# Bias of the fourth attention block added by VectorE instead of by identity matmuls, with a new order of the work

## The chip, the cores and the metric

One core of one Trainium2 chip runs the whole kernel. The metric is the device time of one launch in microseconds (us).

## The reference, cut to what matters

```python
# q, k, v: 4 x 8 heads x 768 x 64; 8 global keys, 96 local ones
scores = scale * np.matmul(q, k.transpose(0, 1, 3, 2))
bias = -slopes[:, None, None] * dist[None, :, :]          # ALiBi-like, per head
scores = np.where(keep, scores + bias, -1e9)              # local band and global keys
a = softmax(scores);  x = a @ v                           # -> 3072 x 512
h = x @ w_in                                              # 512 x 2048: "first product"
out = softplus(h) @ w_out                                 # 2048 x 512: "second product"
```

Attention runs in 24 blocks of 128 queries, each against its own 128 keys and the 128 before (the first block of a sequence against its own alone). The two products run in 12 groups of 256 tokens; group g needs blocks 2g and 2g+1.

## The kernel before: what the change and the argument touch

The kernel is one list of small pieces of work, called ops here. A planner inside it gives each op a duration, a rank and its buffers, and lets the engines take ready ops by rank; the resulting list is emitted, and from then on each engine's order is fixed. `RANKS`, `BASE` and the `slack` of transfers steer the planner. A block with index below `EARLY` gets its bias on TensorE, a later one on VectorE:

```python
def bias_in(n, half, s_t):                    # TensorE: bias into PSUM
    for e in range(2):
        nc.tensor.matmul(s_t[:, 4*e:4*e+nr, :], ident[:],
                         bias[:, half, nr*e:nr*e+nr, :], start=True, stop=False)

def add_bias(n, half, s_t):                   # VectorE: PSUM + bias -> z in SBUF
    nc.vector.tensor_tensor(packed(n, z), rows_of(n, s_t), bias, ALU.add)
# ... (cut)
if n < EARLY:
    bi = pl.add(f"bias{n}{half}", "pe", 0.43 if i else 0.22, ...)
    sc = pl.add(f"scores{n}{half}", "pe", ...)          # adds onto the bias in PSUM
    ex = pl.add(f"exp{n}{half}", "act", 1.05, ...)      # reads PSUM
else:
    sc = pl.add(f"scores{n}{half}", "pe", ...)
    ab = pl.add(f"bias{n}{half}", "dve", 1.22, ...)     # scores + bias
    ex = pl.add(f"exp{n}{half}", "act", 1.05, ...)      # reads z
```

After the exponential come pv (times v, TensorE), norm (VectorE), TX (a transpose, TensorE) and TXout (a copy of the transposed block to XT, by VectorE or ScalarE). TX writes one of the two PSUM banks `h_ps` of the first product (or `o_ps`), so TXout both gives the products their input and frees a bank. ScalarE's exponential of a first product's result frees its bank, and its logarithm then makes the input `g` of the second product. `gv` are two small copies of global v rows, on VectorE, per half block at first and per block from block 4 on. And w_in comes in four slices, each of which serves two of a group's eight first products; the third slice is issued only at about 24 us.

The softmax here doesn't subtract the row's maximum and nothing guards it: scores larger than these inputs give would overflow.

## Time and profile before

| | before |
|---|---|
| time, median of 3 runs | 217.98 us (217.66 to 218.1) |
| span of the profile | 216.0 us |
| TensorE / VectorE / ScalarE busy | 97% / 56% / 72% |
| first product starts | 19.39 us |
| TensorE waits over 0.15 us after that | none |

The lines that carry this are in the prediction. One view is added here: the busy time of each engine in the stretch from 19.4 to 33 us (columns: stretch, its length, then busy us and count of instructions of TensorE, its weight loads, VectorE, ScalarE and GpSimd, then clock, DMA share and GB/s).

```profile
19.40:33.00 13.60, 13.60 (x148) 10.53 (x149) 8.48 (x21) 11.38 (x17) 4.80 (x7) 1.00 1.11 224
```

### The profile page before, as it was taken

Reading aid. Unit: us, or ns where it says so; the run is one execution under the profiler, and the core shown is the slowest. Engines: PE = TensorE matmul, PEld = TensorE weight load, DVE = VectorE, ACT = ScalarE, POOL = GpSimd, SP = SyncE. Lnnn points to the kernel's source line nnn. Section 1 sums busy time; section 2 is a strip of 40 time slices with the busy share of each in tenths; the row PEclk is TensorE's granted clock in tenths of the full one; section 3 lists DMA queues with packets and bytes.
Section 4 is the critical chain, followed back from the end, with each engine's and each line's share of the span. In section 5 each row is a group of like instructions: output and inputs, shape, how many; then the busy total and the mean of one; then the engine's idle time right before and its main releaser. Section 6 shows DMA issues by size and latency. Waiting matters only on the chain.

```text
span 216.0 us, 5102 instructions
## 1 busy us (share of the span) xinstructions
PE 210.3 (97%) x2060; PEld 146.1 (68%) x2060; DVE 122.0 (56%) x258; ACT 156.4 (72%) x208; POOL 65.2 (30%) x125
## 2 busy tenths in 40 slices
PE   8898999999999999999999999999999999999994
PEld 7576786766675767677767767666666766676643
DVE  6888664578837784883653854653774763111020
ACT  2667988887785869979869669749859768766530
POOL 3642710023965090560523271460550000000000
DMA  5999999999996999698988457767963211410112
GB/s 182 328 227 206 267 192 203 272 287 294 232 170 148 319 119 253 164 148 198 153 213 246 133 134 227 210 102 179 261 77 97 74 28 49 76 42 6 52 49 97
DMA packets 69879, 36.24 MB, mean 168 GB/s; under 512 B 28512, under 2 KB 67680, under 8 KB 69856
## 3 DMA queue, kind: packets, MB, share of 16 engines
q1 hardware_dynamic: 64528, 28.39, 57.5%
q0 software_dynamic: 5184, 7.34, 15.9%
q8 instruction: 16, 0.26, 0.6%
q10 hardware_dynamic: 144, 0.20, 0.3%
q14 instruction: 7, 0.06, 0.1%
HBM read 27.26 MB, written 6.29 MB: 155 GB/s over the span
## 4 chain that ended last, share of the span: by engine, by line
PE 91%; DMA 3%; DVE 2%; ACT 1%; SPq 1%; issue 0%
PE h_ps L591 40%; PE o_ps L619 32%; PE s_ps L492 6%; PE x_ps L547 5%; DMA q<-in_q_dram 3%; PE s_ps L644 3%; PE s_ps L619 3%; PE o_ps L732 1%; PE h_ps L418 1%; PE s_ps L477 1%; DVE vb L401 1%; DVE kb L370 0%; SPq L358 0%; PE o_ps L644 0%; PE x_ps L544 0%
## 5 line engine op out<-in xcount | busy, mean ns | idle before, releaser
L591 PE MATMUL h_ps<-XT,w_in_bf 128*128 128x256 bf16 x768 | 95.9, 273 | 0.8 <-DVE rcp L558 0.7
L591 PEld LDWEIGHTS <-w_in_bf 128*128 128x128 bf16 x768 | 72.9, 98 | 19.5 <-issue 1.1
L602 ACT ACTIVATE e<-h_ps 128x512 f32<-128x512 f32 x96 | 58.8, 629 | 33.8 <-PE h_ps L591 33.3
L619 PE MATMUL o_ps<-w_out_bf,g 128*128 128x512 bf16 x320 | 79.6, 379 | 0.0
L610 ACT ACTIVATE g<-e 128x1024 bf16<-128x1024 f32 x48 | 50.6, 1054 | 0.8
L619 PEld LDWEIGHTS <-g 128*128 128x128 bf16 x352 | 32.1, 98 | 26.1
L523 DVE TENSOR_TENSOR z<-s_ps,biasA 128x1024 f32<-128x1024 f32 x34 | 40.6, 1220 | 14.5 <-PE s_ps L492 13.9
L529 ACT ACTIVATE pb<-z 128x1024 bf16<-128x1024 f32 (+1 forms) x40 | 39.3, 984 | 7.0 <-DVE z L523 6.9
L558 DVE RECIPROCAL rcp<-x_ps 128x4 f32<-128x4 f32 x47 | 8.5, 180 | 37.9 <-PE x_ps L547 35.7
L663 DVE COPY osb<-o_ps 128x512 f32<-128x512 f32 x20 | 13.7, 685 | 23.6 <-PE o_ps L619 23.5
L401 POOL CAST vb<-v 64x512 bf16<-64x512 f32 (+1 forms) x39 | 23.4, 601 | 5.9 <-DMA v<-in_v_dram 3.9
L401 POOL CAST kb<-k 64x512 bf16<-64x512 f32 x32 | 20.6, 644 | 15.0 <-DMA k<-in_k_dram 13.7
L559 DVE TENSOR_TENSOR xs<-x_ps,rcp 128x256 bf16<-128x256 f32 x47 | 19.9, 424 | 1.6
L547 PEld LDWEIGHTS <-pb 128*128 128x128 bf16 x320 | 14.7, 97 | 3.4
L547 PE MATMUL x_ps<-vb,pb 128*128 128x65 bf16 x312 | 15.9, 193 | 0.0
L461 POOL COPY kT<-kT 128x32 bf16<-128x32 bf16 x12 | 2.5, 209 | 36.2 <-PE s_ps L492 26.7
L492 PEld LDWEIGHTS <-kT 64*128 64x128 bf16 x288 | 8.3, 94 | 7.5 <-issue 7.4
L669 POOL DMA_DIRECT2D out_dram<-osb x12 | 6.8, 568 | 18.7 <-DVE osb L663 16.8
L470 DVE COPY vb<-vb 4x512 bf16<-4x512 bf16 (+1 forms) x36 | 11.8, 328 | 0.5
L492 PE MATMUL s_ps<-qT,kT 64*128 64x128 bf16 x288 | 12.0, 218 | 0.0
L732 PE MATMUL o_ps<-zeros 128*128 128x128 bf16 x84 | 8.7, 261 | 1.4 <-DVE zeros L687 1.0
L533 ACT ACTIVATE pb<-s_ps 128x1024 bf16<-128x1024 f32 (+1 forms) x8 | 7.4, 920 | 3.0 <-PE s_ps L492 3.0
(79 smaller groups left out, 111.5 us busy)
## 6 DMA issues: line engine op xcount, KB each, us to landing
q<-in_q_dram SPq DMA_DIRECT2D x8, 512.0 KB, 5.6
k<-in_k_dram SPq DMA_DIRECT2D x8, 512.0 KB, 7.3
v<-in_v_dram SPq DMA_DIRECT2D x7, 512.0 KB, 7.9
out_dram<-osb POOLq DMA_DIRECT2D x12, 256.0 KB, 4.5
out_dram<-osb SPq DMA_DIRECT2D x11, 256.0 KB, 2.1
v<-in_v_dram SPq DMA_DIRECT2D x10, 256.0 KB, 3.4
w_in_bf<-in_moe_w_in_dram POOLq DMA_DIRECT2D x4, 512.0 KB, 8.8
w_out_bf<-in_moe_w_out_dram POOLq DMA_DIRECT2D x4, 512.0 KB, 11.7
```

The source lines that it names most:

```text
L401: copy_on[eng](dst[64 * r : 64 * r + 64, hs, :], src)
L470: nc.vector.tensor_copy(vb_of(n - 1)[sl, hs, 0:D], vb_of(first)[sl, hs, 0:D])
L492: nc.tensor.matmul(s_t[:, 4 * sub + (lh // 2 if i == 0 else 2 * (lh // 2) + b), :], k_of(n - b, rows, m), q_of(n, rows, m), start=begin, s ...
L523: nc.vector.tensor_tensor(packed(n, z), rows_of(n, s_t), bias, ALU.add)
L529: nc.scalar.activation(pb[:, 0:nr, :], z[:, 0:nr, :], AF.Exp, scale=1.0 / root_d)
L547: nc.tensor.matmul(xv[:, lh, :], pb[:, 2 * j + b, :], vb_of(n - b)[:, h, :], start=b == 0, stop=b == 1,)
L559: nc.vector.tensor_tensor(xs[:, 4 * half : 4 * half + 4, :], xv[:, :, 0:D], rcp[:][:, :, None].to_broadcast([P, 4, D]), ALU.mult,)
L591: nc.tensor.matmul(hv[:, j, :], w_in_bf[:, m, fb * P : fb * P + P], XT[:, m, W * g : W * g + W], start=(m == 0), stop=(m == NM - 1),)
L602: nc.scalar.activation(e[:, p % 2, :].rearrange("p (a t r) -> p a r t", a=4, r=2), state["h", g, p][:].rearrange("p (a r t) -> p a r t", a ...
L610: nc.scalar.activation(gt[:, 4 * c : 4 * c + 4, :].rearrange("p a t -> p (a t)"), state["e", g, c][:].rearrange("p a t -> p (a t)"), AF.Ln ...
L619: nc.tensor.matmul(dst, state["g", g][:, fb, ns * P : ns * P + P], w_out_bf[:, fb, :], start=(fb == 0), stop=(fb == NFB - 1),)
L663: copy_on[eng](osb[:], src)
```

## The change

The intent: take 0.86 us of matmuls that only add a bias off the full engine and give them to an engine with idle time. The diff, cut to its core:

```diff
 RANKS = {
-    ... 43 entries ...
+    ... 52 others ...
 }
-EARLY, MERGED, T_DMA, X_DMA = 4, 6, 4, 6
+EARLY, MERGED, T_DMA, X_DMA = 3, 6, 4, 6
-BASE = (-29.37, -38.43, -34.65, -17.24, 5.3, 14.23, -7.79, -35.22, 17.37, ...)
+BASE = (-42.8, -42.7, -41.18, -41, -13.51, 14.08, 7.53, -8.91, 17.37, ...)
-            slack=2.5 if w >= 4 else 0.0,                 # loads
+            slack=2.2 if w >= 4 else 0.0,
-            ... slack=2.4 ...                             # both transposes by DMA
+            ... slack=2.0 ...
```

## The prediction

> **What bounds the kernel now.** I read the head of the page first, to see which engine has no idle time. The three rows are busy time, then the busy tenths of 40 slices of 5.4 us.
>
> ```profile
> PE 210.3 (97%) x2060; PEld 146.1 (68%) x2060; DVE 122.0 (56%) x258; ACT 156.4 (72%) x208; POOL 65.2 (30%) x125
> PE   8898999999999999999999999999999999999994
> DVE  6888664578837784883653854653774763111020
> ```
>
> TensorE is at nine tenths in every slice but the first three (8, 8, 9, 8) and the last. VectorE has its densest stretch in slices 2 to 4 (5 to 22 us), and much room later. Busy alone proves little for TensorE, since matmuls overlap in the record, so next I read the waits of TensorE from 19.4 to 206 us, and then the mean step from the start of one matmul to the next in the timeline. The waits have one line in all:
>
> ```profile
> PE h_ps L591 <- DVE rcp L558: 0.7, 1, 0.7
> ```
>
> That is the wait that ends at 19.39 us, where the first matmul of the feed-forward part starts. After it TensorE never waits. The steps agree: the first product (128x256) takes 0.109 us a matmul and the second (128x512) 0.216 us, all through. So from 19.39 us on the time is the sum of the TensorE work that is left: the last matmul piece starts at 212.16 and runs 0.91, so the matmuls end at 213.07, and 213.07 - 19.39 = 193.7 us are saturated. The rest of the 216.0 us span is a tail of 2.9 us (copy and store). Everything that this change can win lies in two places: less TensorE work after 19.39 us, or a better use of the time before it.
>
> The second place I read from the timeline of TensorE (start, duration, what ran):
>
> ```profile
> 15.25 0.39 PE L732 MATMUL o_ps<-zeros 128*128 128x128 bf16 x4
> 15.57 0.40 PE L492 MATMUL s_ps<-q_first,k_first 64*128 64x128 bf16 x8
> ...
> 17.47 0.59 PE L477 MATMUL s_ps<-biasA,ident 128*128 128x512 bf16 x2
> 17.90 0.41 PE L547 MATMUL x_ps<-vb,pb 128*128 128x65 bf16 x8
> 18.24 0.40 PE L492 MATMUL s_ps<-q_first,k_first 64*128 64x128 bf16 x8
> 19.39 1.03 PE L591 MATMUL h_ps<-XT,w_in_bf 128*128 128x256 bf16 x8 [0.75 <-DVE rcp L558]
> 20.26 0.41 PE L547 MATMUL x_ps<-vb,pb 128*128 128x65 bf16 x8
> 20.50 0.59 PE L477 MATMUL s_ps<-biasA,ident 128*128 128x512 bf16 x2
> 20.93 0.41 PE L547 MATMUL o_ps<-vb,pb 128*128 128x65 bf16 x8
> ```
>
> L732 are fillers: products of zeros that keep TensorE awake and yield nothing. Between the first useful data (6.15) and 19.39 us I add the steps taken up by fillers: 0.27, 0.90 (with a gap in it), 0.24, 0.35, 0.42, 0.17, 0.32, 0.33, 0.29, 0.32 = 3.61 us. Add the idle pieces before 8.39 (0.44) and before 19.39 (0.75): 4.8 of these 13.24 us are no work. They are not free for the taking: each is there because the next block's data had not come through its casts, copies and exponentials. What they say is that before 19.4 us the limit is latency, and that it runs through VectorE: the chain of waits has VectorE pieces back to back from 16.35 to 19.34 us, where it does two casts of v, two small copies and then the copy to XT that the first product waits for.
>
> **What the Trainium skill says.** "TensorE: Matmul & The Clock Gate", Back-to-back issue gap, gives 518 cycles for N = 512 and 262 for N = 256, at 2.4 GHz: 0.216 and 0.109 us. The trace agrees: the bias matmuls step by 0.215, the two products by 0.216 and 0.109. "VectorE: DVE Perf Modes", The TRN2 errata, gives (N + 151)/0.96 ns for an fp32 add of two tensors, 1224 ns for N = 1024; the trace has 1220 ns for the same add of scores and bias. "Perfetto Trace Analysis", Optimization Strategy, notes that a kernel can have several regimes whose most-contended engine changes; here these are the 19.4 us of latency and the 194 us of TensorE.
>
> **The change part by part.** EARLY goes from 4 to 3, so the block with index 3 no longer gets its bias by matmuls.
>
> 1. *Removed from TensorE.* Each half has two 128x512 bias matmuls: 2 x 0.215 = 0.43 us, 0.86 us for both. The group has 12 such matmuls, six calls: blocks 1, 2 and 3, two halves each. By order of start the last two, at 17.47 and 20.50 us, are block 3's. The one at 20.50 lies in the saturated stretch: **-0.43 us** goes straight to the end. The one at 17.47 lies before the 0.75 us wait, and by itself would only lengthen that wait. It counts only if the new order puts other useful work there, or if the order has moved block 3 past the wait; I give it half, **-0.2 us**.
>
> 2. *Added to VectorE.* Two adds of scores and bias. The group that does it for the later blocks:
>
> ```profile
> L523 DVE TENSOR_TENSOR z<-s_ps,biasA 128x1024 f32<-128x1024 f32 x34 | 40.6, 1220 | 14.5 <-PE s_ps L492 13.9
> ```
>
> 2 x 1.22 = 2.44 us. ScalarE's exponential stays as it is, about 1.0 us, reading the sum from SBUF and not from PSUM. Block 3's scores come at 18.24 and 21.27 us in the kernel before. Counting busy time, VectorE has 2.1 us idle in 20 to 25, 1.25 in 25 to 30 and 2.7 in 30 to 35 us, so 2.44 us fit once the first product has started. Before 19.4 us it has little: 3.7 busy of 4.9 us from 14.5 to 19.4. If the add falls there, ahead of the XT copies of blocks 0 and 1, the first product starts up to 1.22 us later per add, and TensorE then has only fillers to run.
>
> 3. *Latency of block 3.* One VectorE step more per half, about 1.3 us. Block 3's output is needed only for the second group of the first product. The eight pieces of group 0 start at 19.39, 21.84, 22.77, 23.88, 27.26, 28.58 (two of them) and 30.76; group 1 starts only at 34.91. Block 3's transpose runs at 24.87, ten us early. The latency is hidden: 0.
>
> 4. *Moved.* All base times of the first eight blocks and nearly all ranks change, so this is another order, planned for the new work. The first four blocks get times well ahead of everything (-43 to -41), blocks 6 and 7 move back. The margins for DMA landings in the plan shrink (2.4 to 2.0, 2.5 to 2.2 us). I expect the order to win some of the 4.8 us: the 0.75 us wait, or a few fillers by bringing block 3's work before the first product. A search had been made for the kernel before too, so I estimate **-0.6 us**, within 0 to -1.5. For smaller margins, where a transposed block may come a little late for its matmul, I estimate **+0.1 us**.
>
> Sum: -0.43 - 0.2 - 0.6 + 0.1 = -1.1 us. 217.98 - 1.1 = **216.9 us**, -0.5%.
>
> **The rivals.**
> - *VectorE takes the place of the wait.* The 2.44 us land in the stretch of 14 to 22 us, where it is the engine that releases the first product. For it: slices 2 to 4 of its row (8, 8, 8), and the chain from 16.35 on. Against it: the planner gives each add its duration, and has been searched with it; the casts of v and the copies to XT may go to other engines (ScalarE is 4.1 busy of 4.9 us there, GpSimd 1.95). If it came true: up to +1.2 us for one add on the chain, less 0.4 to 0.9: 217.6 to 218.8.
> - *The bias matmuls were hidden anyway.* They ran instead of fillers, so their removal gives more fillers and no time. For it: one of the two lies before a wait, and fillers still appear after 22.7 us. Against it: the other lies where TensorE never waits; the fillers after 19.4 us take only 0.17 us. It would make -0.4 at most: 217.6 to 218.0.
> - *The new order is the larger part.* If it brought the start of the first product forward by 1 us with the same work ahead of it, or exchanged 1.5 us of fillers for attention work, the time would be 215.5 to 216. For it: 4.8 us of no work. Against it: the arrival of q and k, which no order changes, the start of the loads being untouched (the chain waits on a DMA of q until 8.97), and the search made before.
> - *A stall later on.* The margins are smaller, so transposes by DMA may come late between 50 and 160 us. For it: DMA queues are busiest in slices 1 to 16. Against it: TensorE had no wait at all there, and VectorE and ScalarE run ahead. +0.3 to +1 us if it happens.
>
> **Range and chances.** The three runs before spread by 0.44 us. The sure part is -0.43, the fourth rival spoils it by some tenths, the second leaves -0.2, the third gives -2. Eight in ten: 215.7 to 218.2. Faster by over 2% would take -4.4 us, nearly all of the 4.8 us of no work: 0.03. Slower by over 2% would take a new repeated stall: 0.01. Within 2%: 0.96.
>
> **What the changed profile would show.** (1) The group of 128x512 bias matmuls has 8 and not 12, the VectorE adds with biasA 36 and not 34, all near 1.22 us. (2) TensorE's busy time falls by about 1 us and stays at nine tenths after 20 us, with no wait over 0.3 us later. (3) The first product starts between 18.5 and 19.6 us, with less time in fillers before it. (4) The tail after the last matmul is again 2.9 us. The prediction is wrong if the first product starts past 20.5 us (VectorE on the chain), if the steps of the later matmuls grow, or if waits of TensorE on transposed q, k or XT appear; it is also wrong, to the good side, if most fillers between 9 and 19 us are gone.

## The result, and the profile after

| | before | after |
|---|---|---|
| time, median | 218.0 us (217.66 to 218.1, 4 runs) | 219.16 us (219.1 to 219.33, 4 runs) |
| ratio, 95% interval | 1 | 1.0057 (1.004 to 1.0075) |
| span of the profile | 216.0 us | 217.4 us |
| first product starts | 19.39 us | 19.43 us |

Ratios here and below are the mean time of one kernel's fast runs over that of the kernel before in the same rounds, so not quite the ratio of the medians quoted beside them. The change costs 0.6% where I had predicted a gain of 0.5%; 219.16 us is outside my range.

The head of the changed kernel's page, to set beside that of the kernel before (busy time, then the busy tenths of 40 slices):

```profile
PE 208.5 (96%) x2037; PEld 146.6 (67%) x2069; DVE 125.0 (58%) x259; ACT 156.8 (72%) x208; POOL 66.5 (31%) x126
PE   8799989999999999999999999999999999999994
DVE  6878795657746955984654855643954753110020
```

By this view nothing has happened: TensorE is as full as before, VectorE at 58% and not 56%. Even the drop of TensorE's busy time by 1.8 us is no gain, since 32 matmul records are lost from this trace (2037 matmuls, 2069 weight loads). The removed work is gone: the bias has 12 weight loads in all and not 16. VectorE has its two adds more:

```profile
L525 DVE TENSOR_TENSOR z<-s_ps,biasA 128x1024 f32<-128x1024 f32 x36 | 42.9, 1220 | 9.5 <-PE s_ps L494 8.7
```

The same stretch as above, of the changed kernel:

```profile
19.40:33.00 13.60, 12.71 (x153) 10.02 (x155) 11.46 (x26) 9.81 (x13) 5.39 (x8) 1.00 1.15 230
```

VectorE went from 8.48 to 11.46 us of 13.60. TensorE fell from 13.60 to 12.71, and 0.94 us of those 12.71 are fillers. Its waits from 19 us on, which had one line before (0.7 us, the start of the first product):

```profile
PE h_ps L593 <- DVE XT L580: 1.1, 2, 0.8
PE o_ps L621 <- issue: 0.2, 1, 0.2
```

The first line holds the start of the first product (0.30 us) and a second wait that is new. (The other line stands where a matmul record is lost, and I make nothing of it.) The timeline of TensorE shows where it stood (start, duration, what; idle before in brackets):

```profile
22.97 0.39 PE L571 MATMUL h_ps<-ident,xs 128*128 128x128 bf16 x4
23.19 0.94 PE L734 MATMUL o_ps<-zeros 128*128 128x128 bf16 x14
23.98 1.89 PE L621 MATMUL s_ps<-w_out_bf,g 128*128 128x512 bf16 x7
...
27.26 0.39 PE L571 MATMUL o_ps<-ident,xs 128*128 128x128 bf16 x4
27.65 0.61 PE L420 MATMUL h_ps<-ident,kb 128*128 128x128 bf16 x8
29.06 1.05 PE L593 MATMUL h_ps<-XT,w_in_bf 128*128 128x256 bf16 x8 [0.80 <-DVE XT L580]
```

Two losses. From 23.19 to 23.98 us TensorE runs fillers, because the second product has no input yet (ScalarE's logarithm makes it from 22.72 to 23.78) and block 2's transpose at 22.97 came 1.37 us later than in the kernel before (21.60). The kernel before has two more first products to run while that logarithm is made (at 22.77 and 23.88). At 29.06 a first product waits for VectorE's copy of block 3 to XT. Measured from start to start (the last transposes need 8 x 0.056 us), that wait is 29.06 - 28.10 = 0.96 us.

The sum, against the kernel before: bias matmuls in the saturated stretch -0.43; fillers after 19.4 us 0.79 against 0.17, so +0.62; the wait +0.96; the start of the first product +0.04. Together +1.19 of the 1.40 us by which the span grew. The other 0.2 us I could not pin to one place, as the two orders of work differ.

VectorE of the changed kernel just before that wait:

```profile
26.70 0.68 DVE L394 CAST kb<-k 128x1024 bf16<-128x1024 f32 x1
27.30 1.24 DVE L472 COPY vb<-vb 4x512 bf16<-4x512 bf16 x2
28.58 0.42 DVE L580 COPY XT<-o_ps 128x512 bf16<-128x512 bf16 x1
28.92 0.75 DVE L435 COPY kT<-h_ps 128x512 bf16<-128x512 bf16 x2
```

It is back to back: VectorE, half idle on the average of the span, is the engine that sets the pace just before this wait. In the kernel before, the pair of small copies and the copy of block 3 to XT were these:

```profile
24.64 0.65 DVE L470 COPY vb<-vb 4x512 bf16<-4x512 bf16 x2
25.32 0.42 DVE L578 COPY XT<-o_ps 128x512 bf16<-128x512 bf16 x1
```

### The profile page after: what moved, and what is told of

The parts are those of the page before. It is cut to its first block, busy times and chain, and to the rows that moved or that the text cites. A ratio compares the mean times of both kernels' runs of the same rounds, so it can differ in the third digit from the quotient of the medians.

```text
span 217.4 us, 5082 instructions
## 1 busy us (share of the span) xinstructions
PE 208.5 (96%) x2037; PEld 146.6 (67%) x2069; DVE 125.0 (58%) x259; ACT 156.8 (72%) x208; POOL 66.5 (31%) x126
## 3 DMA queue, kind: packets, MB, share of 16 engines
HBM read 27.26 MB, written 6.29 MB: 154 GB/s over the span
## 4 chain that ended last, share of the span: by engine, by line
PE 89%; DVE 7%; issue 2%; ACT 1%; POOL 0%; POOLq 0%; DVEq 0%
PE h_ps L593 39%; PE o_ps L621 30%; PE s_ps L494 6%; PE x_ps L549 4%; PE s_ps L621 3%; PE s_ps L646 3%; DVE vb L472 1%; PE o_ps L734 1%; DVE bias L726 1%; DVE xs L561 1%; DVE z L525 1%; DVE biasA L731 1%; PE h_ps L571 1%; ACT k_first L387 1%; PE x_ps L546 0%
## 5 line engine op out<-in xcount | busy, mean ns | idle before, releaser
L621 PE MATMUL o_ps<-w_out_bf,g 128*128 128x512 bf16 x294 | 75.4, 379 | 1.4 <-issue 0.2
L525 DVE TENSOR_TENSOR z<-s_ps,biasA 128x1024 f32<-128x1024 f32 x36 | 42.9, 1220 | 9.5 <-PE s_ps L494 8.7
L531 ACT ACTIVATE pb<-z 128x1024 bf16<-128x1024 f32 (+1 forms) x42 | 41.4, 990 | 6.8 <-DVE z L525 6.7
L403 POOL CAST vb<-v 64x512 bf16<-64x512 f32 (+1 forms) x40 | 24.6, 616 | 7.7 <-DMA v<-in_v_dram 5.8
L472 DVE COPY vb<-vb 4x512 bf16<-4x512 bf16 (+1 forms) x36 | 13.3, 369 | 0.5
L734 PE MATMUL o_ps<-zeros 128*128 128x128 bf16 x97 | 9.3, 255 | 1.5 <-DVE zeros L689 1.0
L734 PEld LDWEIGHTS <-zeros 128*128 128x128 bf16 x97 | 7.7, 117 | 2.7 <-issue 1.2
```

What stands on the lines that cost most here:

```text
L403: copy_on[eng](dst[64 * r : 64 * r + 64, hs, :], src)
L472: nc.vector.tensor_copy(vb_of(n - 1)[sl, hs, 0:D], vb_of(first)[sl, hs, 0:D])
L531: nc.scalar.activation(pb[:, 0:nr, :], z[:, 0:nr, :], AF.Exp, scale=1.0 / root_d)
L621: nc.tensor.matmul(dst, state["g", g][:, fb, ns * P : ns * P + P], w_out_bf[:, fb, :], start=(fb == 0), stop=(fb == NFB - 1),)
L734: nc.tensor.matmul(o_ps[:, 0:P], zeros[:], zeros[:])
```

## The experiments

The question is which of three things costs: **the adds on VectorE** (their time on the engine, theory A1; or the longer way of block 3 from scores to exponential, A2), **the new order** (B), or some third engine or transfer. Because the order is fixed once emitted, most experiments keep one kernel's order op by op and change one thing in it. For those, I compared the start of every weight load of TensorE (idle-time fillers and bias left out) with the load of the same number in the kernel it came from. A delay then shows as a step at one load. (A first load can run some tenths ahead of its matmul; at the bias matmuls I go by the loads and matmuls after it.) Each was timed in five rounds. In the three sets of runs the kernel before had medians of 217.58, 218.04 and 217.96 us; compare ratios across sets with care.

### 1. Order and bias, each alone

Run after_again is the changed kernel once more, as the measure for its neighbours.

> The changed kernel unaltered, as the common measure for the runs beside it: 219.1 to 219.3 us, ratio 1.005 to 1.006 to the kernel before.

Measured: 218.79 us (218.44 to 219.07), ratio 1.0046 (1.0029 to 1.0062). As expected in ratio.

Run b_dve3: the kernel before, op by op, but block 3's bias on VectorE.

```diff
-  lambda op: bias_in(n, half, s_of(op))
+  lambda op: None if n == 3 else bias_in(n, half, s_of(op))
-  lambda op: expo_early(n, half, s_of(bi))
+  lambda op: (add_bias(n, half, s_of(bi)), expo(n, half)) if n == 3 else expo_early(...)
```

> The kernel before in its own order of work; only block 3's bias goes to VectorE (two adds of 1.22 us, emitted where ScalarE's exponential stood), four bias matmuls fewer. Theory A (the adds push VectorE's other work of blocks 2 and 3 back by 1.2 us each, TensorE runs out of work after 21 us): 218.3 to 219.0. Theory B (the new order is at fault, not the adds): 0.4 us are saved, 217.5 to 217.7.

Measured: 219.86 us, ratio 1.0112 (1.0083 to 1.0141), worse than even theory A said. That ratio is too high: three of the six runs had a lower granted clock (0.983 to 0.992) and took 220.16 to 221.5 us. The three at 0.999 to 1.000 took 219.54 to 219.56 us, which is 1.0083 of the mean of the kernel before (217.75), still above theory A. Why this run alone met the lower clock is open. The steps against the kernel before: it is 0.31 us ahead from 9 us on, by chance, and just as much at the first product, so the pair of bias matmuls missing ahead of it only made its wait longer, as the prediction had said of this pair by itself. Then it loses 1.14 us at a pv that waits for block 3's exponential (it starts at 21.75 where the kernel before has 20.93), and 0.8 us at a first product:

```profile
19.95 0.41 PE L547 MATMUL x_ps<-vb,pb 128*128 128x65 bf16 x8
21.75 0.42 PE L547 MATMUL o_ps<-vb,pb 128*128 128x65 bf16 x8 [1.40 <-ACT pb L529]
...
24.36 1.03 PE L591 MATMUL h_ps<-XT,w_in_bf 128*128 128x256 bf16 x8 [0.60 <-DVE XT L578]
```

Run a_pe3: the changed kernel, op by op, but block 3's bias back on TensorE.

```diff
-  lambda op: scores(n, half, s_of(op), True)
+  lambda op: (bias_in(...), scores(n, half, s_of(op), False)) if n == 3 else scores(...)
-  lambda op: add_bias(...)
+  lambda op: None if n == 3 else add_bias(...)
```

> The changed kernel in its new order; only block 3's bias goes back to four identity matmuls, the two adds are gone from VectorE. Theory A (the adds cost): VectorE is 2.4 us freer, block 2's transpose runs 1.2 us earlier, the fillers near 23 us and most of the 0.96 us wait near 28 us go, 0.43 us of matmuls come back: 217.8 to 218.4. Theory B (the order is at fault): 219.5 to 219.7.

Measured: 219.36 us, ratio 1.0071 (1.0055 to 1.0087). Theory A misses. Theory B holds by the ratio, at its lower edge (219.5 us is 1.0070 of the 217.98 that I started from), though not by the median. The four cases, all on one chip in the same rounds:

| ratio to before | old order | new order |
|---|---|---|
| bias on TensorE | 1 | 1.0071 |
| bias on VectorE | 1.0112; at full clock 1.0083 | 1.0046 |

So it is not the one or the other. With the bias on VectorE the new order is better than the old one by 0.4% at full clock: it repairs a little under half of what the adds break. With the bias on TensorE the new order is 0.7% worse than the old: it has the repair built in. And within the new order the move does pay: the mean with the bias on VectorE is 0.55 us below a_pe3 (218.76 against 219.31), about the matmuls saved. In a_pe3 the 14 fillers are still there, because ScalarE still ends the logarithm only at 24.26 us, and the wait for the XT copy is still 0.61 us, though VectorE has no add of block 3 and even waits for TensorE:

```profile
21.63 0.46 DVE L472 COPY vb<-vb 4x256 bf16<-4x256 bf16 x2 [1.12 <-PE o_ps L549]
```

```profile
23.67 0.94 PE L734 MATMUL o_ps<-zeros 128*128 128x128 bf16 x14
29.35 1.05 PE L593 MATMUL h_ps<-XT,w_in_bf 128*128 128x256 bf16 x8 [0.61 <-DVE XT L580]
```

So in the changed kernel the fillers and most of that wait belong to the order. An order that runs block 3 late does so even when its bias isn't late.

### 2. VectorE's time, or block 3's longer way?

Run b_dummy: the kernel before with all its bias matmuls, plus two adds of the same size that nobody reads, where b_dve3 has its adds.

```diff
+  def busy_dve(n):
+      if n == 3: nc.vector.tensor_tensor(t[:], biasA[:, 0], biasA[:, 1], ALU.add)
-  lambda op: expo_early(n, half, s_of(bi))
+  lambda op: (busy_dve(n), expo_early(n, half, s_of(bi)))
```

> The kernel before, all bias by matmuls, plus two adds of 128x1024 on VectorE that nobody reads, at the places where b_dve3 has the two adds of block 3 (so VectorE has the same 2.4 us more, but block 3's chain is no longer by itself). Theory A1 (what costs is VectorE's time: block 1's and 2's normalise and copies come later): most of b_dve3's loss stays, 218.9 to 220.0. Theory A2 (what costs is the longer way of block 3 from scores through the add to the exponential): 217.6 to 218.1.

Measured: 219.22 us (219.20 to 219.24) against 218.04, ratio 1.0039 (1.0014 to 1.0065). Here block 3's own way is untouched, and 0.85 us are still lost by the ratio. The run is 0.30 us ahead at the first product and loses that and 0.09 us more at a pv that waits for a small copy of v behind the first dummy add. Most of the loss is in one place, a step from +0.09 to +1.46 us, which stays to the end of the matmuls. TensorE and VectorE there:

```profile
22.79 0.22 PE L737 MATMUL o_ps<-zeros 128*128 128x128 bf16 x1
24.23 1.03 PE L596 MATMUL h_ps<-XT,w_in_bf 128*128 128x256 bf16 x8 [1.21 <-DVE XT L583]
```

```profile
22.62 1.22 DVE L528 TENSOR_TENSOR busy<-biasA 128x1024 f32<-128x1024 bf16 x1
23.75 0.42 DVE L583 COPY XT<-h_ps 128x512 bf16<-128x512 bf16 x1
```

The same copy and the same first product in the kernel before:

```profile
22.30 0.41 DVE L578 COPY XT<-h_ps 128x512 bf16<-128x512 bf16 x1
```

```profile
22.77 1.04 PE L591 MATMUL h_ps<-XT,w_in_bf 128*128 128x256 bf16 x8
```

A first product of group 0 needs no data of block 2, whose copy this is; what the copy releases is its `h_ps` bank. The 1.22 us add stands ahead of a 0.42 us copy that frees a bank, and TensorE waits 1.21 us. So A1 is shown by itself. A2 is shown as a part: at the pv where b_dve3 loses 1.14 us for an exponential that stands behind the add, b_dummy, whose exponential does not, loses 0.39.

Runs b_dve_h0 and b_dve_h1: b_dve3 with the first or the second half alone (`n == 3 and half == 0`, or `1`).

> The kernel before in its own order; only the first half of block 3's bias goes to VectorE (one add of 1.22 us, two matmuls fewer, those ahead of the wait for the first product). From the trace of b_dve3, where TensorE lost 1.34 us at the product that waits for this half's exponential: 218.6 to 219.0. If that loss only stood in for the later one: 217.6 to 218.2.

Measured: 218.66 us, ratio 1.0041 (1.0022 to 1.006), in the first range. At the first product the run is 0.26 us ahead, then it loses 1.14 us at the pv that waits for the exponential, and it ends the matmuls 0.89 behind. (The 1.34 of the expectation was read at a load that ran ahead.)

> The same with the second half alone (its two matmuls lie where TensorE never waits, so 0.43 us are saved for sure; the add goes ahead of block 2's copy to XT on VectorE). If the prediction's first step holds by itself (0.43 us straight to the end): 217.2. If the add, by holding that copy and the exponential back, makes TensorE wait as in b_dve3 (0.6 us and more): 218.0 to 218.8.

Measured: 218.75 us, ratio 1.0039 (1.002 to 1.0058), at the upper end of the second range. This run is the prediction in small. The saving is there: TensorE is 0.21 us ahead at the first product and 0.64 us ahead once it has passed the place of the missing matmuls. At the next but one first product it is 0.92 us behind, at the same bank:

```profile
22.22 0.22 PE L732 MATMUL o_ps<-zeros 128*128 128x128 bf16 x1
23.68 1.03 PE L591 MATMUL h_ps<-XT,w_in_bf 128*128 128x256 bf16 x8 [1.25 <-DVE XT L578]
```

### 3. Relieving VectorE in the changed kernel

Run a_gvlater: the pair of small copies (L472 above) goes behind the copy to XT. (`gv4` is that pair.)

```diff
+    move("gv4.0", "after", "TX3out.0")     # in the emitted list
```

> The changed kernel; on VectorE alone the two small copies of v of the first block (1.24 us together) are put behind block 3's copy to XT, not ahead of it. If the wait of TensorE that ends at 29.06 us is for that copy, it falls from 0.96 us to 0.2 or less: 218.3 to 218.6. If another thing holds that matmul (weights, the transposed k): 219.1 to 219.2.

Measured: 218.93 us, ratio 1.0055 (1.0035 to 1.0074): no gain. (The profile is of the slowest of its six runs, 219.67.) Not because the wait was for something else: it is gone, and the product starts at 28.17 and not 29.06. But VectorE's queue is not shorter, so the next two things that TensorE needs of it come late:

```profile
28.17 1.03 PE L593 MATMUL h_ps<-XT,w_in_bf 128*128 128x256 bf16 x8
29.85 0.23 PE L494 MATMUL s_ps<-qT,kT 64*128 64x128 bf16 x2 [0.64 <-DVE kT L435]
...
32.76 0.24 PE L494 MATMUL s_ps<-qT,kT 64*128 64x128 bf16 x2 [0.66 <-DVE z L525]
```

Gained 0.91 us, lost 0.72 and then 0.65. Moving one job of VectorE moved the wait to the next.

Run a_castdve: a cast of v (GpSimd, 27.78 us, 0.61 us) goes to VectorE, after the first add of block 4.

```diff
-  {"dve": ..., "pool": ...}        # castv of window 2
+  {"dve": 0.42}
```

> The changed kernel; one cast of v (0.61 us, GpSimd, at 27.8 us) goes to VectorE, behind the adds of block 4. If the pair of small copies on VectorE at 27.3 us is long (1.24 us, not the 0.60 of the pairs with GpSimd idle) because that cast ran beside it, the pair takes 0.6 to 0.7 us and the wait before 29 us falls by 0.5: 218.2 to 218.5. If not, 218.8 or more (VectorE has 0.42 us more).

Measured: 218.88 us, ratio 1.0034 (1.0008 to 1.006). The pair took 0.80 us and the wait before the product 0.55 us, so the direction is as expected; the time is not (218.2 to 218.5), and against the changed kernel the gain is within the noise. Better evidence came unasked. In the profile of after_again, the same program, the v transfer landed later and the cast started only at 27.98 us:

```profile
27.28 0.80 DVE L472 COPY vb<-vb 4x512 bf16<-4x512 bf16 x2
28.11 0.42 DVE L580 COPY XT<-o_ps 128x512 bf16<-128x512 bf16 x1
```

The pair ran 0.80 us and not 1.24, the XT copy came 0.47 us earlier, the product 0.47 us earlier (28.59), and the whole rest of the run with it. Over all pairs of 4x512 in the traces of before and after, those without a GpSimd cast beside them take 0.58 to 0.65 us and those with one 0.90 to 1.40. The Trainium skill, "SBUF — State Buffer", SBUF: two separate sides, says that GpSimd and some VectorE instructions take one shared pair of ports as a lock for the whole instruction. These traces agree in that the pair lengthens, by 0.3 to 0.8 us, beside casts of 0.6 us each; that the lock is the reason, and which of the two held it, they do not show.

Run a_gvpool: the small copies of blocks 2, 3 and 4 go to GpSimd altogether; those of block 4 are also emitted later, behind the last load of w_out.

```diff
-  nc.vector.tensor_copy(vb_of(n - 1)[...], vb_of(first)[...])
+  (nc.gpsimd if n in (2, 3, 4) else nc.vector).tensor_copy(...)
```

> The changed kernel; the same small copies go to GpSimd, some 2.6 us off VectorE between 13 and 29 us. Theory A1 (VectorE is the limit from 19 to 32 us there): block 2's transpose about 0.9 us earlier, the wait near 28 us gone: 217.6 to 218.2. If VectorE is not the limit: 218.8 as after_again.

Measured: 219.14 us, ratio 1.0039 (1.0014 to 1.0063), so the time missed the expectation. The trace met it as far as the wait that it named: against the changed kernel TensorE is 0.81 us ahead at the first product and 1.67 us ahead at the product near 28 us. Then it gives 0.85 back in a new wait of 0.86 us, at 31.48, for VectorE's add of block 4, and 0.3 at 50 us, within the scores of block 6 (for what, the profile does not show).

Part of the miss lies outside the profile's span (from the first to the last instruction). The time of a run less its span is 1.7 to 1.8 us in all runs without copies of `vb` on GpSimd, but 2.2 to 2.3 us here and in a_gvpool2: the mean span is 1.0019 of that of the kernel before, the mean time 1.0040. No run shows what the added 0.45 us are.

Run a_gvpool2 tried to remove that new wait, which I put down to three casts of v on VectorE (1.92 us and not 1.30) meeting the copies on GpSimd.

> a_gvpool with the first block's two small copies behind GpSimd's cast of v and not ahead of it. In a_gvpool TensorE was 1.67 us ahead of the changed kernel at the 29 us wait and lost 0.85 of it in a new wait for VectorE's add of block 4, whose casts of v ran beside those copies (1.92 us for three, not 1.30). If that meeting made the new wait, it shrinks to 0.3 or less and the run is 0.5 us below a_gvpool's ratio (1.0039): ratio 1.000 to 1.002. If VectorE's queue alone makes it: 1.0035 to 1.0045.

Measured: 220.11 us (218.94 to 220.48), ratio 1.009 (1.0067 to 1.0114). A miss: the wait is again 0.86 us and the three casts again 1.92 us, so which of GpSimd's jobs they meet made no difference here. The profile was taken of the fastest run (218.94) and shows nothing that explains the slower ones, whose spans are longer too (217.4 to 218.3 against 216.7); that stays open.

### 4. The same relief in the kernel before

Run b_gvpool makes the two edits of a_gvpool in the kernel before.

> The kernel before; the small copies of global v of blocks 2, 3 and 4 go from VectorE to GpSimd (2.5 us off VectorE between 14 and 26 us). If VectorE's queue sets the start of the first product, it starts about 0.45 us earlier than 19.39: 217.1 to 217.4. If latency elsewhere does: 217.6; slower if GpSimd holds the weights' transfers up.

Measured: 218.31 us against 218.04, ratio 0.9995 (0.9968 to 1.0022). The first product starts 0.61 us earlier (18.78); 0.45 us of it is left at 50 us. The time outside the span is 1.8 to 1.9 us here.

Run b_gvpool23 moves only the copies of blocks 2 and 3.

> The kernel before; only the small copies of blocks 2 and 3 go to GpSimd, the first block's stay on VectorE. The first product starts 0.6 us earlier as in b_gvpool. If what follows is bound by TensorE's work, 0.4 us are won: 217.2, ratio 0.998. If the loads of the later blocks hold it: ratio 0.9995 to 1.0005.

Measured: 217.78 us (217.68 to 218.81) against 217.96, ratio 1.0000 (0.9979 to 1.002). Its median is 0.2 us below; the interval does not let me call it faster. By the trace the first product starts 0.39 us earlier (not 0.6), and that is kept to the end of the matmuls; the median span is 215.75 against 216.2 us. But the time outside the span is 2.0 to 2.1 us and not 1.7 to 1.8, as above. No run beat the kernel before clear of noise.

## Why the prediction was wrong, point by point

1. **Removed from TensorE, -0.43 us: right; -0.2 us for the other pair: not there.** b_dve_h1 shows the first: from 0.21 to 0.64 us ahead, across the place where the two matmuls were. The pair ahead of the wait gave nothing: b_dve3 is as far ahead at the first product as long before it (0.31), and the changed kernel starts it 0.04 us later.
2. **Added to VectorE, "2.44 us fit once the first product has started": wrong, and this is the step that failed.** The size was right (1220 ns each) and the sum of idle time was right. But I added up idle time in 5 us windows and took it for room. In the old order, on which I worked this out, the move cost 1.8 us (b_dve3 at full clock), where I had -0.6. From 19.4 to 25 us VectorE went from 3.51 to 5.30 us busy of 5.60 in the changed kernel. Idle time of an engine that others wait for is room only where no waiting copy stands behind the new work. A 1.22 us add ahead of a 0.42 us copy cost TensorE 1.21 us (b_dummy) and 1.25 us (b_dve_h1).
3. **"The latency is hidden: 0": wrong.** I counted the first eight pieces of the first product as group 0. The emitted list of the kernel before says otherwise: the pieces at 19.39, 21.84, 22.77 and 23.88 are group 0's, those from 27.26 on are group 1's, and the other four of group 0 come only from 34.91 on. So block 3 is needed at 27.26 us, not at 34.91: its copy to XT ran at 25.32, with 1.5 us to spare, not ten. In the changed kernel the copy runs at 28.58. And within the block a pv waits at once for the exponential (1.14 us lost in b_dve3).
4. **The order, -0.6 us: near in size beside the moved bias, but no gain on the kernel before.** With the bias on VectorE the new order gains 0.8 us on the old one (219.55 us at full clock to a mean of 218.76). That goes into repairing the move and leaves 1.0 us of its 1.8. On the bias by matmuls the same order costs 1.56 us (a_pe3). Whether another order would keep the saving and lose less is open. The smaller margins for transfers did no visible harm: TensorE has no wait for a q, k or XT transposed by DMA in the changed kernel.

Of my rivals the first came nearest, VectorE taking the place of the wait, and I had even sized it (up to 218.8). I looked for it in the wrong stretch, ahead of the first product, where the start hardly moved (19.43). It came 2 to 5 us after it in the runs in the old order, and 10 us after it in the changed kernel.

Of my signs, the adds (36 at 1220 ns), the start of the first product and the tail (2.9 us) came as said. The fillers before it did not fall: counted alike they took 3.87 us and not 3.61. A TensorE wait over 0.3 us did appear, and it was on XT, which I had named as a sign of being wrong. One reading was loose: TensorE's row has its 8s in slices 1, 2 and 4, not in the first three.

One thing about how the order was made can be read from the emitted lists, which hold planned starts:

```
                               before    after
planned end of matmuls          212.74   212.66
measured end of matmuls         213.06   214.46
planned TensorE gaps, 46-82 us    0.72     none
product that waits for block 3's XT copy in the changed kernel:
  planned 26.81, run 29.06 (2.25 late; the ops just before it 1.5 to 1.6 late)
```

By its plan the change was to be 0.08 us shorter. The plan charges the kernel before with 0.72 us of gaps after 46 us which its profile does not have, and it lets the changed kernel's product start 0.7 us sooner, relative to its neighbours, than it did. Some 0.6 of these 0.7 us are the pair of small copies on VectorE ahead of that copy, planned at 0.62 us and run in 1.24. The two, less the 0.08, are about the 1.40 us between the measured ends. That the search chose this order because of them is my inference; no run shows it.

## What to carry to other kernels

Before moving work to an engine with idle time, list what stands behind the place where it would go in that engine's queue, and who waits for it: buffer releases count, not only data. The share of busy time, even by window, does not answer that; a dummy of the same length at the same place shows the part that is the engine's time, in one run. Where the order of work was searched, judge a change with its order and without, since each order carries the waits that it was made for.

## What the Trainium skill lacked or had wrong

- "TensorE: Matmul & The Clock Gate", Back-to-back issue gap, gives some 131 ns a matmul for N = 512 in a stream of weight loads and matmuls, and calls its 216 ns the isolated case. Here the stream of the second product, each matmul with its own weight load, steps by 216 ns throughout.
- "GPSIMD Engine Reference", Engine selection, says that operations with one input are roughly at line rate on GpSimd. It does not say how short bf16 copies compare. Here they took about twice as long there as on VectorE: a pair of 4x256 took 0.83 to 0.96 us on GpSimd in all but two cases (1.13 each), and 0.44 to 0.48 on VectorE; a pair of 4x512 took 1.45 to 1.51 on GpSimd, and 0.58 to 0.65 on VectorE with no GpSimd cast beside it.
- "SBUF — State Buffer", SBUF: two separate sides, has the lock of the shared ports but no figure for a stream of small VectorE copies beside GpSimd casts. The runs: a pair of 0.6 us takes 0.90 to 1.40 us.
- No page that I found says how to tell, before a change, whether an engine's idle time is room when another engine waits on buffers that it frees. "Perfetto Trace Analysis", Identifying the Most-Contended Engine, goes by occupancy for VectorE (the page does say, under Optimizing Scalar/DVE Operations, that an engine that isn't saturated can cause bubbles on others); VectorE at 56 to 58% of the span delayed TensorE by 1.2 us.
